# A finer dependency cell for the last output store, and a memory update that shares a PSUM bank with the product with V

## The chip, the core and the metric

The kernel runs on one core of a Trainium2 chip. The metric is device time in microseconds (us) of one execution. Engines: PE is TensorE's matmul, PEld its weight load, DVE is VectorE, ACT is ScalarE, POOL is GpSimd, SP the sync engine, which issues every DMA of this kernel. A DMA *lands* when its completion is signalled. A *bank* is one of the eight slices of PSUM (`PS` in the code, 128 x 8 x 512 in f32) that the matmuls write; an *eviction* copies a result out of it.

## The reference, cut to what matters

A pre-layernorm attention block with a compressive memory, followed by a gated MLP, on 2048 tokens of width 1024 with 32 heads. The 2048 tokens are four segments of 512. In every segment:

```python
logits = einsum('bhqd,bhkd->bhqk', qs, ks) * scale + mask      # causal, inside the segment
a_dot  = softmax(logits) @ vs
a_mem  = phi(qs) @ M / (phi(qs) @ z + 1e-6)                    # memory of the segments before; phi(t) = t + 1 if t > 0 else exp(t)
o      = g * a_mem + (1 - g) * a_dot
M, z   = M + phi(ks).T @ vs, z + phi(ks).sum()                 # the memory update
```

In the first segment M and z are zero, so phi(q) is not needed there. The block's output goes through `wo`, a residual, a layernorm and the MLP, and the result is stored row block by row block.

## The kernel before: the parts that matter

The attention loop has 32 *steps* (4 segments of 8 groups of 4 heads). Step n computes the logits of group n in three rounds, works on the product with V ("PV"), normalization and memory update of group n-1, and on the projections for n+1. Cut to what matters:

```python
for n in range(32):
    s, c = divmod(n, 8)
    logits(n, 0)                       # "first logits", banks 0-3; then ACT: first exponential
    fill(f1)                           # K projection of n+1, next bank of the rotation
    if n > 0:
        pv(n - 1, range(3) if s == 3 else range(4))   # banks 4 and 5; ends with norm(n-1)
    logits(n, 1)                       # "second logits", banks 0-3 again, second exponential
    if s == 3: pv(n - 1, (3,))
    if n > 0: state(n - 1)             # memory update
    bg_pop()                           # layernorm work: bn_stats on DVE, and so on
    fill(f2)                           # Q projection of n+1
    logits(n, 2)                       # "third logits" (+ product with the memory)
    phi_exp(n + 1)                     # ACT
    fill(f3); phi_max(n + 1); bg_pop(); fill(f4)      # V or output projections
```

Two banks, 6 and 7, rotate among K, memory update, Q, f3 and f4. The memory update and the normalization:

```python
def norm(n):                                   # all on DVE
    dve.reciprocal(RD[:], PVA[:, :, :, 32])
    dve.tensor_tensor(RD[:], RD[:], OMG[...], ALU.mult)
    ...
    dve.tensor_tensor(TA[:], PVA[:, :, :, 0:32], rb, ALU.mult)
    dve.tensor_tensor(ot, TA[:], TM[n % 2][:], ALU.add)        # "otok"; later segments only

def state(n):
    b = next_bank()
    for tcl in range(4): pe.matmul(PS[:, b, 0:132], PK[n % 3][:, tcl, :], V[...], ...)
    dve.tensor_copy(UPD[n % 2][:], PS[:, b, 0:132])            # "upd", then POOL adds it to M
    ...

def phi_views(n):
    lo = 1 if s == 0 else 0                    # slot 0 is Q, slot 1 is K
    return QK[n % 2][:, lo:hi, :], ...
```

A recorder derives every wait from the cells that an operation touches: 32 bytes in SBUF, a whole bank in PSUM, and 1024 bytes in DRAM. An output row has 2048 bytes. The last row block is stored in three pieces: columns 0 to 511, 512 to 895 and 896 to 1023.

The softmax here doesn't subtract the row's maximum and nothing guards it: scores larger than these inputs give would overflow.

## Time and profile before

| | before |
|---|---|
| median of the first 3 runs | 799.41 us (799.39 to 799.5) |
| profiled execution, span | 797.3 us |
| PE busy | 790.4 us, 99% |
| DVE, ACT, POOL busy | 47%, 37%, 21% |

From the page of the kernel before (busy time by engine, and the chain that ended last):

```profile
PE 790.4 (99%) x5657; PEld 378.9 (48%) x5657; DVE 377.3 (47%) x745; ACT 295.5 (37%) x347; POOL 170.6 (21%) x329
...
PE 96%; DVE 2%; ACT 1%; issue 0%; DMA 0%; DVEq 0%
```

The kernel is bound by PE: only what makes PE wait, or lengthens the start or the end, costs anything. But the ends of matmuls are modelled and overlap, so 99% busy hides small stalls. I therefore read the *start* times of successive matmuls in the trace. In the steady state a 128x512 matmul starts every 0.216 us, and whenever PE goes from full-array matmuls to the 32-row ones of the logits or back, another 0.09 to 0.10 us passes. What exceeds that is a stall. The waits of the kernel before name the largest ones:

```profile
PEld ps L209 <- DVE upd L209: 1.1, 2, 0.6
PE ps L209 <- DVE upd L209: 0.9, 2, 0.5
```

(Columns: time in all, how often, the longest.) The timeline of step 20 shows one of the two. Columns are start, duration, engine, line, operation, out<-in, shape, count, and in brackets the idle time before it with its releaser:

```profile
198.29 0.69 DVE L209 TENSOR_TENSOR ta<-ps,rd 128x512 f32<-128x512 f32 x1
199.02 0.69 DVE L209 TENSOR_TENSOR otok<-ta,tm 128x512 bf16<-128x512 f32 x1
...
199.62 0.29 DVE L209 COPY upd<-ps 128x132 f32<-128x132 f32 x1
...
199.97 1.04 PE L209 MATMUL ps<-wo,oT 128*128 128x512 bf16 x4 [0.47 <-DVE upd L209]
```

The output projection wants the bank of the memory update. That bank is free only when "upd" has been copied out, and the copy stands in DVE's queue behind "otok".

The end of the kernel before, in its timeline (SPq lines are DMA issues, merged):

```profile
792.43 3.26 SPq L209 DMA_DIRECT2D out_dram<-fin  x3
793.10 0.56 DVE L209 TENSOR_TENSOR fin<-fin,ps 128x384 bf16<-128x384 bf16 x1 [0.69 <-PE ps L209]
793.88 0.29 DVE L209 TENSOR_TENSOR fin<-fin,ps 128x128 bf16<-128x128 bf16 x1 [0.23 <-PE ps L209]
```

and the waits of its DMA queue:

```profile
SPq L208 <- DMA out_dram<-fin: 1.3, 1, 1.3
```

The last addition ends at 794.17, but the issue of the last store ends only at 795.69. In between the sync engine waits 1.3 us for the *landing* of the neighbouring store.

### The profile page before, as it was taken

The numbers are of one execution on the slowest core, as the hardware profiler recorded it, in microseconds if no ns is written. First come the engines' busy times: TensorE is split into PE (matmuls) and PEld (weight loads), VectorE is DVE, ScalarE is ACT, GpSimd is POOL, SyncE is SP. The second block draws the span as 40 slices with busy tenths as digits, with TensorE's granted clock in tenths as the row PEclk, the third lists the DMA queues.
The fourth block names the chain that finished last, engine by engine and source line by source line (L and its number), as shares of the span: only waits on it lengthen the run. The fifth ranks groups of instructions, "written<-read, shape, count | busy, mean of one in ns | idle before, by whom it ended". The sixth has DMA issues, their size and how long they took to land.

```text
span 797.3 us, 13127 instructions
## 1 busy us (share of the span) xinstructions
PE 790.4 (99%) x5657; PEld 378.9 (48%) x5657; DVE 377.3 (47%) x745; ACT 295.5 (37%) x347; POOL 170.6 (21%) x329
## 2 busy tenths in 40 slices
PE   8999999999999999999999999999999999999998
PEld 4444455554454455455544444444444444444444
DVE  6764688579844766744562000153233324323432
ACT  5777877787787675133333333100000000000000
POOL 4564565556553331100230000000000000000000
PEclk9999999999999999999999999999999999999999
DMA  9662555363414425411116000740270153021002
GB/s 299 172 166 53 94 81 121 87 107 93 95 27 122 113 65 135 125 47 53 53 54 132 1 1 1 223 87 7 82 129 1 34 122 63 1 67 46 1 8 85
DMA packets 125002, 64.83 MB, mean 81 GB/s; under 512 B 94992, under 2 KB 113936, under 8 KB 124944
## 3 DMA queue, kind: packets, MB, share of 16 engines
q1 hardware_dynamic: 124944, 63.99, 33.0%
q8 instruction: 44, 0.72, 0.4%
q14 instruction: 14, 0.11, 0.0%
HBM read 32.51 MB, written 8.39 MB: 51 GB/s over the span
## 4 chain that ended last, share of the span: by engine, by line
PE 96%; DVE 2%; ACT 1%; issue 0%; DMA 0%; DVEq 0%
PE ps L209 96%; DVE stats L209 1%; ACT e L209 0%; DVE lno L209 0%; DMA xch<-in_A_x_dram 0%; DVE hch L209 0%; DVE ta L209 0%; DVE otok L209 0%; ACT qk L209 0%; DVE rdm L209 0%; DVE mv L209 0%; DVE pqk L209 0%; DVE etmp L209 0%; DVE rd L209 0%; DVE upd L209 0%
## 5 line engine op out<-in xcount | busy, mean ns | idle before, releaser
L209 PE MATMUL ps<-wspT,z 128*128 128x512 bf16 x896 | 194.0, 379 | 0.0
L209 ACT ACTIVATE e<-ps 128x2048 bf16<-128x2048 f32 (+1 forms) x96 | 152.7, 1590 | 49.3 <-PE ps L209 49.2
L209 PEld LDWEIGHTS ps<-wspT,z 128*128 128x128 bf16 x896 | 87.7, 98 | 105.7
L209 DVE TENSOR_TENSOR tmpg<-ps,brow 128x512 f32<-128x512 f32 x56 | 38.7, 691 | 196.8 <-DMA brow<-in_B_b_sp_dram 103.5
L209 POOL TENSOR_SCALAR_AFFINE_SELECT e<-e 128x512 bf16<-128x512 bf16 x128 | 87.9, 699 | 129.5 <-ACT e L209 129.3
L209 PE MATMUL ps<-win,hnT 128*128 128x448 bf16 x512 | 98.3, 352 | 0.0
L209 PE MATMUL ps<-w_out,yT 128*128 128x512 bf16 (+2 forms) x462 | 97.4, 373 | 0.0
L209 PE MATMUL ps<-hnT,win 128*128 128x512 bf16 x448 | 96.9, 379 | 0.0
L209 PEld LDWEIGHTS ps<-win,hnT 128*128 128x128 bf16 x512 | 49.7, 98 | 46.4 <-issue 0.2
L209 PEld LDWEIGHTS ps<-w_out,yT 128*128 128x128 bf16 x462 | 44.7, 98 | 52.3
L209 PEld LDWEIGHTS ps<-hnT,win 128*128 128x128 bf16 x448 | 43.8, 98 | 52.8
L209 PE MATMUL ps<-xnT,wk 128*128 128x512 bf16 x256 | 60.8, 380 | 0.0
L209 PE MATMUL ps<-xnT,wq 128*128 128x512 bf16 x256 | 60.6, 379 | 0.0
L209 PE MATMUL ps<-wv,xnT 128*128 128x512 bf16 x256 | 59.4, 380 | 0.2 <-ACT xnT L209 0.2
L209 PE MATMUL ps<-wo,oT 128*128 128x512 bf16 x256 | 58.0, 379 | 0.9 <-DVE upd L209 0.9
L209 ACT ACTIVATE z<-ps 128x448 bf16<-128x448 f32 x60 | 32.5, 543 | 69.5 <-PE ps L209 69.5
L209 ACT ACTIVATE z1T<-ps 128x512 bf16<-128x512 f32 x56 | 33.4, 597 | 63.3 <-PE ps L209 63.3
L209 DVE TENSOR_TENSOR fin<-fin,ps 128x512 bf16<-128x512 bf16 (+2 forms) x33 | 22.2, 672 | 71.2 <-DMA fin<-out_dram 38.1
L209 DVE BATCH_NORM_STATS2 zst<-z 128x6 f32<-128x448 bf16 x64 | 38.9, 619 | 30.1 <-ACT z L209 30.1
L209 PEld LDWEIGHTS ps<-v,e 128*128 128x128 bf16 x1280 | 37.3, 96 | 9.1 <-issue 1.7
L209 DVE TENSOR_TENSOR yT<-tmpg,z1T 128x512 bf16<-128x512 f32 x56 | 38.7, 692 | 1.9
L209 PE MATMUL ps<-v,e 128*128 128x33 bf16 x1280 | 38.4, 177 | 0.0
(86 smaller groups left out, 608.4 us busy)
## 6 DMA issues: line engine op xcount, KB each, us to landing
xch<-in_A_x_dram SPq DMA_DIRECT2D x16, 256.0 KB, 3.0
xr<-in_A_x_dram SPq DMA_DIRECT2D x16, 256.0 KB, 3.8
out_dram<-hch SPq DMA_DIRECT2D x16, 256.0 KB, 2.4
fin<-out_dram SPq DMA_DIRECT2D x16, 256.0 KB, 2.7
out_dram<-fin SPq DMA_DIRECT2D x31, 128.0 KB, 1.7
win<-in_B_w_in_dram SPq DMA_DIRECT2D x4, 896.0 KB, 5.1
w_out<-in_B_w_out_dram SPq DMA_DIRECT2D x1, 3584.0 KB, 12.7
win<-in_B_w_in_dram SPq DMA_DIRECT2D x3, 1024.0 KB, 5.2
```

The lines of the kernel that those rows point to most:

```text
L209: ins = getattr(e, op.name)(*op.args, **op.kw)
```

## The change

Its intent: the last two stores write different columns, so the second need not wait for the first. And the memory update goes into columns of bank 5, next to the fourth query block of PV, so that it leaves the two-bank rotation. (To free them, the first three query blocks now lie in bank 4; before, each bank had two.) Dependencies go by whole banks, so the update must be multiplied into bank 5 before DVE starts to read that bank. To make room for it, PV runs in two parts around the second logits in every step, and DVE's copy moves ahead of the last addition.

```diff
-            gran = 1024
+            gran = 256
@@
-    PVX = PS[:, 4:6, :].rearrange("p b (h w) -> p (b h) w", w=256)
+    PVX = PS[:, 4:6, :].rearrange("p b w -> p (b w)")[:, 0:688].rearrange("p (q w) -> p q w", w=172)
+    STB = PS[:, 5, 176:308]
@@ pv
-                              start=(cq % 2 == 0 and j == 0 and i == 0), ...)
+                              start=(cq % 3 == 0 and j == 0 and i == 0), ...)
         if 3 in cqs:
+            state(n)
             norm(n)
@@ norm
             dve.tensor_tensor(TA[:], PVA[:, :, :, 0:32], rb, ALU.mult)
+        state_sum(n)                  # the copy out of STB, and POOL's part
+        if s > 0:
             dve.tensor_tensor(ot, TA[:], TM[n % 2][:], ALU.add)
@@ state: the four matmuls go to STB, no next_bank()
@@ main loop
-            pv(n - 1, range(3) if s == NSEG - 1 else range(4))
+            pv(n - 1, range(3))
         logits(n, 1)
-        if s == NSEG - 1:
+        if n > 0:
             pv(n - 1, (3,))
-        if n > 0:
-            state(n - 1)
```

More of the change, by code (lines that the diff above doesn't have):

```diff
@@ L565, in pv @@
                     pe.matmul(PVA[:, cq, i, :], E[n % 2][rnd][:, i, o:o + 128], V[:, j, 4 * c + i, 0:33],
-                              start=(cq % 2 == 0 and j == 0 and i == 0), stop=False, skip_group_check=True)
+                              start=(cq % 3 == 0 and j == 0 and i == 0), stop=False, skip_group_check=True)
         if 3 in cqs:
+            state(n)
             norm(n)
@@ L601, in state, with state_sum @@
         s, c = divmod(n, NQ)
+        for tcl in range(4 if s < NSEG - 1 else 0):
+            pe.matmul(STB, PK[n % 3][:, tcl, :], V[:, tcl, 4 * c:4 * c + 4, 0:33], start=(tcl == 0), stop=(tcl == 3))
+    def state_sum(n):
+        s, c = divmod(n, NQ)
         if s == NSEG - 1:
             return
-        b = next_bank()
-        for tcl in range(4):
-            pe.matmul(PS[:, b, 0:132], PK[n % 3][:, tcl, :], V[:, tcl, 4 * c:4 * c + 4, 0:33],
-                      start=(tcl == 0), stop=(tcl == 3))
         if s == 0:
-            dve.tensor_copy(MSUM[:, c, :], PS[:, b, 0:132])
+            dve.tensor_copy(MSUM[:, c, :], STB)
         else:
-            dve.tensor_copy(UPD[n % 2][:], PS[:, b, 0:132])
+            dve.tensor_copy(UPD[n % 2][:], STB)
             pool.tensor_tensor(MSUM[:, c, :], MSUM[:, c, :], UPD[n % 2][:], ALU.add)
```

## The prediction

> **What bounds the kernel.** TensorE. The page has PE busy 790.4 of 797.3 us (99%); the chain that ended last is 96% PE, 2% DVE. In the timeline of the attention loop (32 steps, 20 to 305 us) I measured the spacing of matmul starts. A 128x512 matmul starts every 0.216 us, and each change between full-array and 32-row matmuls leaves a gap of 0.09 to 0.10 us. The Trainium skill, "TensorEngine Tiling (Array Packing)", section Key Properties, says that a change of tiling mode drains the TensorE; the gap agrees. The change keeps the number of mode changes. Beyond them the loop stalls only 0.22 us in step 0, 0.53 us in each of steps 12 and 20 and 0.075 us in each of steps 14 and 22. In the waits, the large ones of these are "PE <- DVE upd".
>
> **What the change does.**
>
> 1. *Tail.* Dependency cells in DRAM shrink from 1 KB to 256 B, so the last store (columns 896 to 1023) no longer shares a cell with its neighbour (512 to 895). The sync engine's timeline shows the neighbour landing 1.6 us after issue and only then the last store issued, 1.17 us after the DVE addition it needs; it lands 1.5 us later and the kernel ends. Issued right after the addition, both landings overlap. Gain 1.15 us, all on the critical path.
>
> 2. *Memory update leaves the two-bank rotation.* Today its bank is wanted by the next projection, which waits for the DVE copy "upd" behind the whole normalization. Afterwards it sits in bank 5 beside the fourth query block. The four stalls go: 2 x 0.53 + 2 x 0.075 = 1.2 us gained.
>
> 3. *PV in two runs.* The second logits start at 2.75 us of a step instead of 3.15. PE does the same work: step 24, already in the new order, takes 9.427 us against 9.424. Cost 0.003 x 23 = 0.07 us, no gain, because the third logits wait for nothing today beyond the drain.
>
> 4. *Normalization starts later.* Its reciprocal reads bank 5, so it now waits for the last memory-update matmul: 3.94 us into the step instead of 3.26. In segments two and three DVE has slack. In steps 1 to 3 it has not: normalization, copy and two layernorm statistics (0.7 us each) stand before the Q eviction, whose end slips by 0.69 us (6.78 to 7.47). ScalarE's phi exponential then starts at 7.5 instead of 6.81, pushing the V eviction and the next first exponential to an end near 2.85, while the second logits want it by 2.68: about 0.17 us lost in each of steps 2, 3 and 4. Step 8, whose first exponential ends at 2.76 already, loses 0.08. Together 0.6 us.
>
> **Sum.** 799.4 - 1.15 - 1.2 + 0.07 + 0.6 = 797.7 us, a gain of 0.2%. Range 796.9 to 798.6. Within 2%: 0.99; faster: 0.005; slower: 0.005.
>
> **What would show it.** (1) The wait "SPq <- DMA out_dram<-fin" of 1.3 us before the last store is gone. (2) "PE <- DVE upd" is gone; steps 12 and 20 take 9.43 us. (3) Steps 8 to 23 keep 9.42 us. (4) Steps 2 to 4 take 7.77 instead of 7.60 us, with "PEld <- ACT e" before the second logits.
>
> **What would make it wrong.** A later DVE queue in steps 9 to 13 or 17 to 21 stalling the next first logits or K projection; the last store landing slower beside its neighbour; or the early loss being zero (797.1) or doubled.

## The result, and the profile after

The kernel after: 796.83 us median of 6 runs (796.4 to 797.42), beside 799.4 us for the kernel before in its 6 runs (798.81 to 799.5). The ratio is 0.997, 95% interval 0.9957 to 0.9983: real, and far inside "within 2%". (Ratios here are the mean time of one kernel's runs over that of the other's of the same rounds, so they are not quite the ratio of the medians.)

From the page of the kernel after:

```profile
PE 784.7 (99%) x5565; PEld 378.3 (48%) x5657; DVE 380.0 (48%) x745; ACT 295.6 (37%) x347; POOL 173.8 (22%) x329
...
PE 94%; DVE 3%; DMA 2%; issue 1%
```

The lower PE time is no gain: 92 matmul records are missing in this trace (5565 of 5657; the weight loads are complete). The 2% of DMA in the chain is explained below. The end of the kernel after, in its timeline:

```profile
791.61 2.17 SPq L209 DMA_DIRECT2D out_dram<-fin  x3
792.35 0.55 DVE L209 TENSOR_TENSOR fin<-fin,ps 128x384 bf16<-128x384 bf16 x1 [0.77 <-PE ps L209]
793.13 0.29 DVE L209 TENSOR_TENSOR fin<-fin,ps 128x128 bf16<-128x128 bf16 x1 [0.23 <-PE ps L209]
```

The three issues are over 0.36 us after the last addition (793.78 against 793.42) instead of 1.52 us. The sync engine's last wait, for the landing of the last store, ends 1.49 us after the last addition instead of 2.67: a gain of 1.18 us. The wait "SPq <- DMA out_dram<-fin" of 1.3 us is gone, as forecast.

Step 20 of the kernel after, in its timeline:

```profile
198.74 0.69 DVE L209 TENSOR_TENSOR ta<-ps,rd 128x512 f32<-128x512 f32 x1
...
199.30 1.25 PE L209 MATMUL ps<-wo,oT 128*128 128x512 bf16 x5
199.34 0.28 DVE L209 COPY upd<-ps 128x132 f32<-128x132 f32 x1
199.54 0.80 DVE L209 TENSOR_TENSOR otok<-ta,tm 128x512 bf16<-128x512 f32 x1
```

Normalization runs *later* in the step than before, but the output projection starts at 199.30 without a wait, even before the copy. "DVE upd" is gone from the waits of PE. ("otok" itself is longer than before here, 0.80 us, and over 1 us in most steps of segments two and three, because POOL is at work when it starts; see e5. PE waits for none of it.) In its place stands one that I had not predicted:

```profile
PEld ps L209 <- DMA pk<-pqk: 0.9, 1, 0.9
PE ps L209 <- DMA pk<-pqk: 0.8, 1, 0.8
```

It is in step 1, where the first memory update waits for the DMA that transposes the first block of phi(k). (That DMA, 10.9 us from issue to landing, is also the 2% of DMA in the chain.) From the timeline of the kernel after:

```profile
30.51 0.23 PEld L209 LDWEIGHTS ps<-v,pk 128*128 128x128 bf16 x4 [0.86 <-DMA pk<-pqk]
```

Because the loop is so regular, the lengths of the steps can be compared to a few nanoseconds. They are read from the traces (first logits to first logits, us), here for all kernels; the experiments follow below.

| kernel | 1 | 2 to 4 | 8 | 12 and 20 | 14 and 22 |
|---|---|---|---|---|---|
| before | 7.61 | 7.60 | 9.42 | 9.96 | 9.50 |
| after | 8.53 | 7.60 | 9.49 | 9.42 | 9.42 |
| e1_tail_only | 7.82 | 7.60 | 9.42 | 9.96 | 9.50 |
| e2_copy_first | 7.61 | 7.60 | 9.42 | 9.42 | 9.42 |
| e3_no_split | 8.97 | 7.83 | 9.65 | 9.65 | 9.65 |
| e4_after_again | 7.86 | 7.60 | 9.49 | 9.42 | 9.42 |
| e5_split_only | 7.61 | 7.60 | 9.49 | 10.73 | 9.62 |
| e6_copy_last | 8.19 | 7.60 | 9.49 | 9.47 | 9.42 |
| e7_phi_both | 7.94 | 8.19 | 9.49 | 9.42 | 9.42 |
| e8_wq_late | 7.61 | 7.60 | 9.49 | 9.42 | 9.42 |
| e9_short | 7.78 | 7.60 | 9.42 | 9.42 | 9.42 |
| e10_short_wq | 7.61 | 7.60 | 9.42 | 9.42 | 9.42 |
| e11_before_again | 7.61 | 7.60 | 9.42 | 9.96 | 9.50 |
| e12_copy_first_again | 8.54 | 7.60 | 9.42 | 9.42 | 9.42 |

The two profiled executions, 797.3 and 795.4 us, then differ by this account: the loop starts 0.52 us earlier (-0.52), step 1 is 0.92 longer (+0.92), steps 12 and 20 are 0.53 shorter each (-1.07), steps 14 and 22 0.075 each (-0.15), step 8 is longer (+0.07), and the end shorter (-1.18). The sum is -1.93; measured is -1.92. Three of these terms were predicted to size: the end, the four stalls and step 8. The first two terms cancel in part; the experiments show that they are not the change's doing.

### The profile page after: what moved, and what is told of

It is laid out like the page before. It is cut to its first block, busy times and chain, and to the rows that moved or that the text cites. A ratio compares the mean times of both kernels' runs of the same rounds, so it can differ in the third digit from the quotient of the medians.

```text
span 795.4 us, 13019 instructions
## 1 busy us (share of the span) xinstructions
PE 784.7 (99%) x5565; PEld 378.3 (48%) x5657; DVE 380.0 (48%) x745; ACT 295.6 (37%) x347; POOL 173.8 (22%) x329
## 4 chain that ended last, share of the span: by engine, by line
PE 94%; DVE 3%; DMA 2%; issue 1%
PE ps L209 94%; DMA pk<-pqk 1%; DVE stats L209 1%; DMA xch<-in_A_x_dram 0%; DVE hch L209 0%; DVE otok L209 0%; DVE lno L209 0%; DVE pqk L209 0%; DVE ta L209 0%; DVE xnT L209 0%; DVE rd L209 0%; DVE mv L209 0%; DVE etmp L209 0%; DVE rdm L209 0%; DVE upd L209 0%
## 5 line engine op out<-in xcount | busy, mean ns | idle before, releaser
L209 POOL TENSOR_SCALAR_AFFINE_SELECT e<-e 128x512 bf16<-128x512 bf16 x128 | 90.3, 717 | 126.2 <-ACT e L209 125.9
L209 PE MATMUL ps<-xnT,wq 128*128 128x512 bf16 x225 | 53.9, 379 | 1.8 <-issue 0.2
L209 PE MATMUL ps<-v,e 128*128 128x33 bf16 x1280 | 42.2, 178 | 0.0
```

The source lines that it names most:

```text
L209: ins = getattr(e, op.name)(*op.args, **op.kw)
```

## The experiments

All outputs are right.

### e1_tail_only: the smaller cell alone

```diff
-            gran = 1024
+            gran = 256
```

> Kernel before with the smaller DRAM cells alone. Theory A (the last store was issued only when its neighbour had landed): 1.17 us faster than before, about 798.2; the end of the last DVE addition to the last landing takes 1.49 us instead of 2.67; the attention steps are as before, steps 12 and 20 still 9.96 us. Rival B (the DMA queue, not the wait, sets the landing of the last store): under 0.5 us gained.

Measured: 797.8 us median of 5 runs against 799.07, ratio 0.9986 (0.9974 to 0.9999). The interval is wide for so small a gain, so the trace has to decide: from the last addition to the end of the wait for the last landing it takes 1.49 us, as in the kernel after, and the steps are those of the kernel before (step 1 apart). Its end in the timeline:

```profile
791.97 2.18 SPq L209 DMA_DIRECT2D out_dram<-fin  x3
793.50 0.29 DVE L209 TENSOR_TENSOR fin<-fin,ps 128x128 bf16<-128x128 bf16 x1 [0.23 <-PE ps L209]
```

The issues end 0.36 us after the last addition. That is the whole gain of the end, shown by itself. Rival B is out.

### e2_copy_first: only the copy's place in DVE's queue

```diff
 (kernel before)
-            dve.tensor_tensor(ot, TA[:], TM[n % 2][:], ALU.add)     # in norm()
@@ main loop
             state(n - 1)
+            norm_add(n - 1)                                          # the same addition, here
```

> Kernel before, layout, banks and PE order untouched; only on DVE the memory-update copy goes ahead of the last addition of the normalization. Theory A (the four stalls are a place in the DVE queue: the copy stands behind 0.7 us of work that the waiting projection doesn't need): steps 12, 20, 14 and 22 lose their stalls, 1.2 us gained, about 798.2. Rival B (the update must leave the two-bank rotation for that): steps 12 and 20 stay at 9.96 us, 799.4.

Measured: 798.18 us (5 runs) against 799.07, ratio 0.9989 (0.9975 to 1.0002). Steps 12, 14, 20 and 22 take 9.42 us. PE's order, the banks and the rotation are those of the kernel before. The interval includes 1, but the two profiled executions began their loops alike (20.04 and 20.08 us) and differ by 1.2 us. Step 20 in its timeline:

```profile
198.32 0.28 DVE L209 COPY upd<-ps 128x132 f32<-128x132 f32 x1
198.53 0.68 DVE L209 TENSOR_TENSOR otok<-ta,tm 128x512 bf16<-128x512 f32 x1
198.86 1.19 PEld L209 LDWEIGHTS ps<-wo,oT 128*128 128x128 bf16 x7
```

So the stalls were a matter of the order in one in-order queue. Leaving the rotation is *one* cure (e6 below, where the split is kept as well), not the only one, and my prediction had credited the bank alone.

### e3_no_split: PV in one run, the memory update behind it

```diff
 (kernel after)
-            pv(n - 1, range(3))
+            pv(n - 1, range(3) if s == NSEG - 1 else range(4))
         logits(n, 1)
-        if n > 0:
+        if s == NSEG - 1:
             pv(n - 1, (3,))
```

> Kernel after, but the product with V in one run with the memory update behind it, all ahead of the second logits (steps 1 to 23). Theory A (the split is there to make room: the update must come before DVE reads the bank, and ahead of the second logits it delays the second exponential, which has no slack): second logits at 3.40 us of a step, second exponential to 5.73, third logits at 5.80 instead of 5.55, 0.25 us lost in each of 23 steps, about 5.7 us, 802.5. Rival B (ScalarE has slack there, the split is indifferent): 796.9, steps of 9.42 us.

Measured: 802.26 us (5 runs) against 799.07, ratio 1.0041 (1.0028 to 1.0054). Each of the steps 2 to 23 is 0.23 us longer than in the kernel after (step 8: 0.16). In its timeline of step 3 (the middle line is the second exponential):

```profile
46.24 0.40 PE L209 MATMUL ps<-qk 32*128 32x384 bf16 x8
...
46.69 1.88 ACT L209 ACTIVATE e<-ps 128x2048 bf16<-128x2048 f32 x1 [1.29 <-PE ps L209]
...
48.62 0.29 PE L209 MATMUL ps<-qk 32*128 32x256 bf16 x4 [0.15 <-ACT e L209]
```

The second exponential ends at 48.57, and only then can the third logits overwrite its banks. In the kernel before the same wait was satisfied just in time: its second exponential ended 0.07 us before the third logits began. Theory A holds: the split makes room for the memory update. Without it the steps 2 to 23 cost about 5 us more than in the kernel after, and step 1 is longer by 0.4.

### e4_after_again: the kernel after once more

> Kernel after, unchanged, for its spread and a second trace. Theory A (the 0.92 us wait for the first transposed key block in step 1 comes and goes with the landing of the early weight loads): times between 796.4 and 797.4, the wait differs from 0.92 us and the total differs by about as much. Rival B (the change causes it): again 0.9 us in step 1.

Measured: 796.62 us (796.51 to 797.66, 5 runs) against 799.07, ratio 0.9972 (0.996 to 0.9985). Step 1 took 7.86 us this time, not 8.53, and the execution was 0.8 us shorter (0.67 of it step 1, the rest the start): Theory A. The wait also turns up in e1, whose loop has the old order (step 1 at 7.82). So it comes from neither the split nor the new bank.

Its origin can be read from the traces. The loads of the rest of WK and WQ (1.5 MB each) are issued ahead of the first transposition. The longest time to landing of the transpositions ("DMA to landing", the tile view, first before, then after) is that of this first one; the median is 2.4 us:

```profile
DMA to landing us min/median/max: 2.4/2.4/8.3
```

```profile
DMA to landing us min/median/max: 2.4/2.4/10.9
```

In all twelve traces with both loads ahead, this transposition lands 0.4 to 1.3 us after the WQ load does.

How much PE waits then depends on how early PE gets there, and that varies too. The groups of the kernel before and the kernel after, for the transposes of the first layernorm:

```profile
L209 PE MATMUL ps<-ident,lno 128*128 128x128 bf16 x32 | 3.0, 258 | 0.5 <-DVE lno L209 0.5
```

```profile
L209 PE MATMUL ps<-ident,lno 128*128 128x128 bf16 x32 | 2.3, 220 | 0.5 <-DVE lno L209 0.5
```

In the profiled execution of the kernel before the first fourteen of them ran at half the clock: they started every 0.107 us instead of every 0.056. In its trace the full clock comes at about 7.2 us, when these fourteen are nearly over; in e4's at about 4.9 us, ahead of them. The Trainium skill, "TensorE: Matmul & The Clock Gate", Part 1, says why this differs from run to run: the window over which activity is watched is free-running and does not reset when a kernel starts. The traces agree that it differs: the edge lies between 4.5 and 7.6 us in the thirteen that hold it. That the free-running window is the reason no run here shows. Over the fourteen profiled executions, before and after among them, the loop begins either early (19.3 to 19.5 us) or late (19.9 to 20.2), and in each of the five late ones the edge came after 6.8 us. (The trace of the kernel after holds no clock record; its transposes start every 0.056 us from the second on.) Whether the cell size has a part in that was open until e11 and e12.

### e5_split_only: the split without the new bank

```diff
 (kernel before)
-            pv(n - 1, range(3) if s == NSEG - 1 else range(4))
+            pv(n - 1, range(3))
         logits(n, 1)
-        if s == NSEG - 1:
-            pv(n - 1, (3,))
         if n > 0:
+            pv(n - 1, (3,))
             state(n - 1)
```

> Kernel before with the product with V in two runs around the second logits in all steps; bank of the memory update, its copy's place on DVE and the last store as before. Theory A (the split by itself gains nothing, TensorE had no wait there to lose): second logits at 2.75 us instead of 3.15, steps still 9.42 us, steps 12 and 20 still near 9.96, total 799.1. Rival B (the earlier second logits are the gain of the change): over 1 us faster than before.

Measured: 801.12 us (4 runs) against 799.11, ratio 1.0026 (1.0011 to 1.0041). Rival B is out, but Theory A missed too: I had expected no difference, and it is 2 us slower. Steps 12 and 20 grow from 9.96 to 10.73 us. Their stalls on the copy become 1.3 us, as its timeline of step 20 shows:

```profile
200.41 0.94 DVE L209 TENSOR_TENSOR otok<-ta,tm 128x512 bf16<-128x512 f32 x1
201.27 0.28 DVE L209 COPY upd<-ps 128x132 f32<-128x132 f32 x1
201.61 2.06 PEld L209 LDWEIGHTS ps<-wo,oT 128*128 128x128 bf16 x11 [1.34 <-DVE upd L209]
```

With the split, normalization waits for the last quarter of PV and starts 0.4 us later in its step. DVE is nearly full in the steps with output projections (it works 9.0 of the 9.4 us of step 19 in the kernel before), so it still has the delay in the next step: in step 12 the reciprocal starts 4.80 us into the step instead of 4.27, and "otok" takes 0.94 us instead of 0.69. The Trainium skill, "SBUF — State Buffer", section SBUF: two separate sides, says that DVE and GpSimd share a port pair, and that of a DVE instruction with two SBUF inputs, such as "otok", and a GpSimd instruction that reads SBUF, the one that starts first has it for the whole instruction. The fourteen traces agree: the 91 "otok" additions that start while a POOL instruction runs (its mask on the exponentials, "e<-e") take 0.54 us more than what is left of that instruction, 0.79 to 1.17 us in all; the other 245 take 0.68 to 0.69. The account closes: 2 x 0.77 + 2 x 0.13 + 0.07 = 1.9 us. So the split by itself costs 1.9 us. In the kernel after it costs only the 0.07 us of step 8, because no projection waits for the copy any more.

### e6_copy_last: the new bank with the old order on DVE

```diff
 (kernel after, in norm)
-        state_sum(n)
         if s > 0:
             dve.tensor_tensor(ot, TA[:], TM[n % 2][:], ALU.add)
         ...
+        state_sum(n)
```

> Kernel after, but the memory-update copy on DVE again behind the last addition. Theory A (out of the rotation, no projection waits for the copy wherever it stands): steps 12, 14, 20 and 22 stay at 9.42 us, total 796.7 like after. Rival B (the copy's place ahead of the addition gave the gain in after as well): steps 12 and 20 back above 9.9 us, 797.8.

Measured: 797.02 us (4 runs) against 799.11, ratio 0.9975 (0.9961 to 0.9988). The large stalls stay away, as Theory A says. But steps 11, 12, 19 and 20 take 9.47 to 9.48 us: there the K projection waits 0.05 us for the residual addition on DVE ("hch") that still holds its bank. From its timeline of step 20 (of the 0.28 us of idle time, 0.05 are new):

```profile
192.78 0.68 DVE L209 TENSOR_TENSOR hch<-xr,ps 128x512 bf16<-128x512 bf16 x1
193.51 0.76 PEld L209 LDWEIGHTS ps<-xnT,wk 128*128 128x128 bf16 x5 [0.28 <-DVE hch L209]
```

So with the new bank the earlier copy is worth 4 x 0.05 = 0.2 us, not nothing. That is too little for the times to show; the step lengths show it.

### e7_phi_both: the dependency that my prediction had assumed

```diff
 (kernel after)
-        lo = 1 if s == 0 else 0
+        lo = 0
```

> Kernel after, but the phi exponential of the first segment reads Q and K (as in the middle segments) instead of K alone; results unchanged. Theory A (the chain of the prediction fails only because that exponential doesn't read Q in segment one): in steps 1 to 3 the exponential starts when the Q eviction ends, near 7.49 us instead of 6.82, the next first exponential ends near 3.28, and the second logits of steps 2 to 4 come near 3.35 instead of 2.75: 0.6 us lost in each, total 798.5. Rival B (ScalarE alone set the start, DVE's slip never reaches it): steps 2 to 4 stay at 7.6 us, under 797.2.

Measured: 798.79 us (4 runs) against 799.11, ratio 0.9998 (0.9984 to 1.0012). Steps 2 to 4 take 8.19 us, 0.58 more than in the kernel after (0.6 expected); step 0 (6.78 us instead of 6.60) and step 1 (7.94 instead of 7.61 without the DMA's wait) lose some too, which I had not listed. Two lines each from the timelines of step 2, first of the kernel before, then of the kernel after, then of e7_phi_both. "qk" is the eviction of the Q projection, "etmp" the exponential:

```profile
40.38 0.64 DVE L209 TENSOR_TENSOR qk<-ps,rb 128x512 bf16<-128x512 f32 x1
...
41.05 0.62 ACT L209 ACTIVATE etmp<-qk 128x512 bf16<-128x512 bf16 x1
```

```profile
41.45 0.62 ACT L209 ACTIVATE etmp<-qk 128x512 bf16<-128x512 bf16 x1
41.46 0.64 DVE L209 TENSOR_TENSOR qk<-ps,rb 128x512 bf16<-128x512 f32 x1
```

```profile
42.27 0.64 DVE L209 TENSOR_TENSOR qk<-ps,rb 128x512 bf16<-128x512 f32 x1
42.94 1.06 ACT L209 ACTIVATE etmp<-qk 128x1024 bf16<-128x1024 bf16 x1 [0.57 <-DVE qk L209]
```

In the kernel before the exponential follows the eviction by 0.03 us, which looks like a dependency. In the kernel after the two run side by side: there is none. The shape tells it as well: 128x512 is K alone. Only in e7, with both halves (128x1024), does the exponential wait.

### e8_wq_late: the kernel after with the WQ load behind the first transposition

```diff
-    sp.dma_start(WQ[:, :, 256:D], wcols(A_wq, 256, D))
     phi_exp(0)
     phi_max(0)
+    sp.dma_start(WQ[:, :, 256:D], wcols(A_wq, 256, D))
```

> Kernel after, but the 1.5 MB load of the rest of WQ is issued behind the first transposed-key transpose instead of ahead of it. Theory A (that transpose waits in the queues behind the two big weight loads, and runs whose TensorE clock rises early reach the first memory update before it has landed): the transpose lands before 28 us, step 1 takes 7.61 us instead of 7.86 or 8.53, total near 796.3. Rival B (its landing is late for another reason, such as the transpose itself): step 1 unchanged. Risk: the WQ rest lands after 29.4 us and the Q projection of step 1 waits instead.

Measured: 796.93 us (796.81 to 798.33, 4 runs) against 799.11, ratio 0.9977 (0.9964 to 0.9991). The first transposition lands 4.6 us after its issue instead of 10.9, and step 1 takes 7.61 us. But this execution's clock rose late, at about 7.2 us, and with a late start there might have been no wait anyway. The time is not better than the kernel after's. So the times are inconclusive by themselves, and the forecast of 796.3 was missed; e10 has the early start that was lacking here.

### e9_short and e10_short_wq: two small edits, then a third

e9 is the edit of e2 together with that of e1. e10 adds the edit of e8. They were run on another chip.

> Kernel before with two small edits: the smaller DRAM cells, and the memory-update copy ahead of the last addition on DVE; no split, no new banks. Theory A (tail and place in the DVE queue are the whole gain of the change, and the split and the bank only pay for each other): 1.17 and 1.2 us below before, 796.7, equal to after within 0.3; steps 12 and 20 at 9.42 us, step 8 at 9.42 instead of 9.49. Rival B (split and bank give something of their own): over 0.5 us slower than after.

> The kernel of e9_short with the rest of WQ loaded behind the first transposed-key transpose. Theory A (in runs whose TensorE clock rises early, the start gains up to 0.6 us, and step 1 gives part of it back in the wait for that transpose): the transpose lands near 24.4 us, step 1 takes 7.61 us whatever the clock, lowest time near 796.1 (0.3 to 0.5 below the lowest of e9_short), the highest equal to it. Rival B (the later WQ load costs as much elsewhere, as the Q projection of step 1 waiting): no run under 796.5.

Measured against 799.0 us: e9 797.11 us (796.39 to 797.14, 5 runs), ratio 0.9974 (0.9962 to 0.9987); e10 796.36 us (796.27 to 796.82, 5 runs), ratio 0.9969 (0.9955 to 0.9983). The gain of the whole change is thus had without the split and without the new bank, and without the 0.07 us of step 8. In both traces the clock rose before 6 us. e9 shows the wait in step 1 (7.78 us), e10 doesn't (7.61). That is the test which e8 missed: with an early start and the later WQ load there is no wait. The step alone would not show it, since e11 below starts early and has no wait either; the landing does. The first transposition lands at 24.2 us in e10, 5 us before PE wants it, and at 29.5 in e9. Rival B is out, since three of the five runs of e10 lie under 796.5. The forecast of the lowest time was missed: 796.27 is only 0.12 us below e9's lowest, where 0.3 to 0.5 was expected.

e10 has the lowest median of all kernels here. Beside the kernel before it is faster beyond doubt. Beside the kernel after (796.83 and 796.62 in its two sets, not in the same job) the difference of 0.3 to 0.5 us is about as large as the spread of the runs, and by the ratios it is almost none (0.9969 against 0.997 and 0.9972). That it is faster than the kernel after is likely by the mechanism, not shown by the times.

### e11_before_again and e12_copy_first_again: is it chance?

By then the three profiled kernels with 1 KB cells (before, e2, e5) had all begun the loop late, against two of nine with 256 B cells. So the cell size might have had a hand in it. e11 is the kernel before and e12 that of e2, unchanged. They were run on another chip.

> Kernel before, unchanged, for the start of its loop. So far all three profiled kernels with 1 KB cells began the loop late (with the TensorE clock rising near 7 us), and two of nine with 256 B cells. Theory A (the moment of the clock's edge is chance): an early start, 0.6 us earlier than in the first profile of before, is more likely than not in one of this run and the next; with it, a short wait for the first transposition in step 1. Rival B (the cell size sets it): both begin late.

> Kernel of e2_copy_first again, with 1 KB cells, as a second draw for the start of the loop. Theory A (chance): early or late. Rival B (the cell size sets it): late again.

Both began early: the loop of e11 begins 0.68 us earlier than in the first profile of the kernel before, that of e12 0.81 us earlier than in e2's. Rival B is out. In e11 the first transposition landed in time (step 1: 7.61 us), so the short wait that Theory A expected with an early start did not come. In e12 it took 10.9 us, and step 1 took 8.54 us: as long a wait as in the profile of the kernel after, in a kernel with the old cells, the old banks and PV in one run. So both terms, the early start and the wait in step 1, are variation of the start, not the change. Single times, 798.68 us for e11 and 798.32 for e12, decide nothing here.

## Why the prediction was right or wrong

The prediction was 797.7 us, within 2% with 0.99, and a gain of 0.2%. Measured are 796.83 us as the median and a ratio of 0.997, which times 799.4 is 797.0. The class was right; with effects of about 1 us in 800 it could hardly have been wrong. The size was too small: the gain is 2.4 us by the ratio where 1.7 was forecast, and the median lies 0.07 us below the range's low end of 796.9.

1. *Tail, 1.15 us*: right. 1.18 us in the traces of before and after, and the same in e1 alone. The Trainium skill, "DMA: Bandwidth & Descriptors", section Two DMAs through the same engine are not ordered, says that order comes only from waiting on the completion semaphore; so dropping the wait is safe only because the two stores write different columns, and the result was correct.
2. *The four stalls, 1.2 us*: right in size (1.22). The cause was named incompletely. e2 shows that moving the copy ahead of "otok" in DVE's queue is enough of a cure, and e6 that the bank is another.
3. *PV in two runs costs 0.07 us and gains nothing*: right that it gains nothing, but it costs nothing either where PE is the limit (steps 9 to 23, the four stalls apart, are unchanged to 0.003 us). What the prediction missed is that alone it would have cost 1.9 us (e5), and that without it the bank would have cost about 5 us (e3). The parts of the change are tied to each other.
4. *Normalization starts later; 0.17 us lost in each of steps 2, 3 and 4, and 0.08 in step 8*: this is the step that failed. The words were "ScalarE's phi exponential then starts at 7.5 instead of 6.81". The first half was right: the reciprocal starts at 3.93 us of a step, as forecast (3.94), and the end of the Q eviction slips to 7.45 (forecast 7.47). But in the first segment the exponential reads K alone, and it started at 6.81, as before: where ScalarE gets to it, as its third exponential (5.89 to 6.92 us of the step) ends. Steps 2 to 4 took 7.60 us, not the 7.77 forecast. I took two events that followed each other by 0.03 us for a dependency, with the line that says otherwise in the kernel's own code. e7 puts that dependency in, and the loss appears (0.58 us a step; more than 0.17, since the exponential over both halves is also longer). Step 8 lost 0.07, as forecast.

With the three false losses taken out (0.5 us), and the 0.07 us of point 3, the sum would have been 799.4 - 1.15 - 1.2 + 0.08 = 797.1, which the prediction itself names among what would make it wrong ("the early loss being zero"). Part of what remains is the base: 799.4 is the median of three runs, and the later sets of the kernel before have medians of 799.0 to 799.11. All of it is within what the start of the kernel does from run to run: the clock's edge moves the loop by some 0.6 us, and step 1 gives back between 0 and 0.9.

## What to carry to other kernels

Where one engine is saturated, look for its stalls in the spacing of its instructions, not in its busy share; then ask what stands in *front* of the releasing instruction in its in-order queue, because moving one small copy ahead of work that nobody waits for gave the same 1.2 us here as a new bank layout. Two events that touch in the trace are not a dependency until the operands say so: compare shapes and slices before you carry a delay along a chain. And when a change consists of tied parts, run them singly: here one part alone cost 1.9 us, another without its partner lost about 5 us, and two small edits had all of the gain.

## What the Trainium skill lacked or had wrong

- "TensorE: Matmul & The Clock Gate", section Back-to-back issue gap, gives about 131 ns a matmul as the sustained spacing at N=512, and says that its formula of about 216 ns over-counts. Here the 128x512 bf16 matmuls, each with its own weight load, started every 215 or 216 ns (2640 of 2712 successive pairs in the kernel before, and none closer), so the formula held and the sustained figure didn't.
- "TensorEngine Tiling (Array Packing)", Key Properties, says that a change of tiling mode drains the TensorE, but not what that costs. Here it was 0.09 to 0.10 us each way between full-array and 32-row matmuls.
- "DMA: Bandwidth & Descriptors", Anatomy of one DMA, gives about 2.0 us of fixed cost for DMAs issued from GpSimd. For a 32 KB store issued from the sync engine the traces show 1.4 to 1.5 us from issue to landing. What the page doesn't have is how late a small DMA lands behind large ones in the same queues: the first transposition (128 KB) took up to 10.9 us behind 3 MB of loads, 4.6 to 4.8 behind half of them, and the median one 2.4 us.
